# One scatter a head across both halves of the array, fixed score buffers, other row tiles

## The chip, the cores and the metric

The kernel runs on one core of a Trainium2 chip. The metric is the device time of one execution in microseconds. Three executions of the kernel before took 1567.34 us in the median (1565.12 to 1568.61). All traces and profiles here are of one execution on that core.

## The reference

Talking-heads attention (the scores and the attention weights are each mixed over the heads) and then two feed-forward layers, in fp32:

```python
# attention: batch 4, heads 12, sequence 448, head_dim 64
scores = (q @ k.transpose(0, 1, 3, 2)) / sqrt(64)
scores = einsum('bhij,hg->bgij', scores, w_pre)       # mix the 12 heads
attn = softmax(scores, axis=-1)                       # with 1e-9 added to the sum
attn = einsum('bhij,hg->bgij', attn, w_post)          # mix the 12 heads again
x = (attn @ v) laid out as (1792, 768)
# feed-forward, 768 -> 1536 -> 768, then 768 -> 2048 -> 768
x = (sigmoid(x @ w_gate) * (x @ w_val)) @ w_out
h = maximum(x @ w_in, 0)
out = (h * h) @ w_out2
```

## The kernel before

The program has two parts that overlap a little: `attention` (lines 65 to 444) and `mlp` (from line 447 on). The second part multiplies each fp32 matrix as three products of rounded parts (line 692) and keeps TensorE busy without a break once attention is over. The change is in attention alone.

A batch's 448 query rows are cut into four row tiles (`row_tiles`, line 33): 120, 120, 120 and 88 rows. Rows are handled in groups of GI = 10, so that 10 rows x 12 heads = 120 partitions: 12, 12, 12 and 9 groups in the four tiles, 45 a batch, 180 in all.

For each tile, `scores` (line 181) is called once for each of six pairs of heads. TensorE makes the two heads' scores (rows of the tile on the partitions, 448 keys along), ScalarE copies one head and VectorE the other from PSUM to SBUF (tile `e`, three buffers of two heads each), and then DMAs scatter `e` into tile `g`, where the rows of a group and the 12 heads lie on the partitions together: 5 rows x 12 heads = 60 partitions in the lower half of the array (0 to 59) and the other 60 in the upper half (64 to 123). A head has two DMAs, one a half (line 209); each moves 60 rows of 1792 bytes in a full tile, from 60 neighbouring partitions to 5 partitions, at a stride of 12, by 12 columns. Nearly all are issued on SyncE's queue (SP), line 217; some of the first tile's on ScalarE's. The first tile is scattered in two blocks (four columns first; the list `second`, line 375, has the rest). `g` has two buffers, so a tile's scatters wait until the groups of the tile before the last have been read.

The loop over the steps s (line 376 on) takes one group a step. `premix` (line 223, every second step) multiplies two groups of `g` by the pre-mixing weights `wp`, four matmuls a group pair and half; `maximum`, `exponent` and `normal` make the softmax on VectorE, ScalarE and GpSimd; `postmix` (line 269) mixes again; `values` (line 298) multiplies by v when a chunk of two tiles is done. The v tiles come through four buffers by loads on SP's queue (line 295), the fifth and sixth of a chunk when `values` has freed the first two. The results leave by stores on the same queue (line 321). `k` and `q` loads (lines 168, 176) are there as well: SP works its queue in program order.

The scores of a later tile n are spread over the steps by the list `front` (line 338): pair p is due at step a + p (z - a) // 6, where a is two steps before the first group of tile n - 1, and z is LA = 5 steps before the first group of tile n. A pair may also be made earlier, from a on, if the planned TensorE cost leaves room.

`masks` (line 121) and `mixers` (line 145) build the mixing weights once at the start.

Of the kernel before, what the change touches and what calls it, by code (L numbers as in the profile page):

```python
# [7 lines left out]
F32 = mybir.dt.float32  # L8
# [3 lines left out]
ALU = mybir.AluOpType  # L12
# [4 lines left out]
P = 128  # L17
JP = 112
GI = 10
HV = 2  # L20
LAG = 3
LA = 5
NA = 9
HB = GI // 2
HP = P // 2
# [6 lines left out]

def row_tiles(S):

    n = -(-S // (8 * GI)) * 2 * GI
    cuts = [t * n for t in range(4)] + [S]
    return list(zip(cuts, cuts[1:]))


def columns(i0, i1):  # L40

    return 2 * -(-(i1 - i0) // (2 * GI))


def blocks(b, i0, i1):

    n = columns(i0, i1)
    return [(0, 4), (4, n)] if b == i0 == 0 else [(0, n)]
# [16 lines left out]
def attention(tc, q, k, v, w_pre, w_post, xs, B, H, S, D):  # L65
# [10 lines left out]
    nc = tc.nc  # L76
    JT = S // JP
    NP = H // 2
# [3 lines left out]
    for b in range(B):  # L82
        for t, (i0, i1) in enumerate(row_tiles(S)):
            if t % 2 == 0:
                chunks.append([b, i0, i1, len(groups), 0])
            for g0 in range(i0, i1, GI):
                groups.append((len(tiles), g0 - i0, min(GI, i1 - g0), len(chunks) - 1, g0))
            chunks[-1][2] = i1
            chunks[-1][4] = len(groups)
            tiles.append((b, i0, i1 - i0))  # L90
# [3 lines left out]
    GT = IM // GI  # L94
    CM = max(c[2] - c[1] for c in chunks)
    KH = HB * H

    with ExitStack() as ctx, ExitStack() as mid, ExitStack() as left:
        kw = dict(side="right")
# [2 lines left out]
        po = ctx.enter_context(tc.tile_pool(name="a_o", bufs=4, **kw))  # L102
        pp = ctx.enter_context(tc.tile_pool(name="a_p", bufs=1, **kw))
        pa = mid.enter_context(tc.tile_pool(name="a_a", bufs=NA, **kw))
        pg = mid.enter_context(tc.tile_pool(name="a_g", bufs=2, **kw))
        ps_b = ctx.enter_context(tc.tile_pool(name="ps_b", bufs=2, space=PSUM, **kw))
        ps_q = mid.enter_context(tc.tile_pool(name="ps_q", bufs=2, space=PSUM, side="left"))
        ps_m = mid.enter_context(tc.tile_pool(name="ps_m", bufs=4, space=PSUM, side="left"))
# [3 lines left out]
        p0 = left.enter_context(tc.tile_pool(name="a_0", bufs=1, side="left"))  # L112
# [4 lines left out]

        wr = p0.tile([P, 2, H], F32, name="wr")
        mask = p0.tile([P, GI, H], F32, name="mask")

        def masks():
            nc.gpsimd.memset(wr, 0.0)
            nc.gpsimd.memset(mask, 0.0)
            nc.gpsimd.memset(wp, 0.0)
            for n, w in enumerate((w_pre, w_post)):
                for u in range(2):
                    nc.sync.dma_start(
                        out=wr[u * HP : u * HP + KH, n, :],
                        in_=w.unsqueeze(0).to_broadcast([HB, H, H]),
                    )  # L130
            for u in range(2):
                m = mask[u * HP : (u + 1) * HP, u * HB : (u + 1) * HB]
                nc.gpsimd.memset(m, 1.0)
                for base, mult in ((0, 1), (H - 1, -1)):
                    nc.gpsimd.affine_select(
                        out=m,
                        in_=m,
                        compare_op=ALU.is_ge,
                        fill=0.0,
                        base=base,  # L140
                        pattern=[[-mult * H, HB], [0, H]],
                        channel_multiplier=mult,
                    )

        def mixers():
            for u in range(2):
                r = slice(u * HP, (u + 1) * HP)
                x = wp[r, :KH].rearrange("p (i g) -> p i g", g=H)
                nc.vector.tensor_tensor(
                    out=x,  # L150
                    in0=mask[r, u * HB : (u + 1) * HB],
                    in1=wr[r, 0:1, :].to_broadcast([HP, HB, H]),
                    op=ALU.mult,
                )
            nc.vector.tensor_scalar(out=wp, in0=wp, scalar1=SCALE, scalar2=None, op0=ALU.mult)
            nc.vector.tensor_tensor(
                out=wq.rearrange("p g i -> p i g"),
                in0=mask,
                in1=wr[:, 1:2, :].to_broadcast([P, GI, H]),
                op=ALU.mult,  # L160
            )
# [17 lines left out]
        g_t, second = {}, []  # L179

        def scores(n, p):

            b, i0, rows = tiles[n]
            isz = full[n]
            if p == 0:
                g_t[n] = pg.tile([P, GT, S], F32, tag="g", name="g")
            kt = k_t.pop((b, p)) if i0 + rows == S else k_t[b, p]
            ps = [
                ps_q.tile([P, S], F32, tag="q", name="ps_s")
                for _ in range(2)  # L190
            ]
            for o in range(2):
                r = slice(o * D, (o + 1) * D)
                nc.tensor.matmul(  # L194
                    ps[o][:isz], lhsT=q_t[n][r, p, :isz], rhs=kt[r], start=True, stop=True
                )
            if n == 0 and p >= 3:
                e = [pa.tile([IM, S], F32, tag="a", name="e0") for _ in range(2)]
            else:
                t = p4.tile([IM, 2, S], F32, tag="e", name="e")  # L200
                e = [t[:, o] for o in range(2)]
            for o in range(2):
                if o:
                    nc.vector.tensor_copy(e[o][:isz], ps[o][:isz])
                else:
                    nc.scalar.copy(e[o][:isz], ps[o][:isz])  # L206
                e0 = 0
                for m, (g0, g1) in enumerate(blocks(b, i0, i0 + rows)):
                    for y in range(2):
                        e1 = e0 + (g1 - g0) * HB  # L210
                        to = g_t[n][y * HP : y * HP + KH].rearrange("(r h) g j -> h r g j", h=H)
                        move = (to[2 * p + o, :, g0:g1], e[o][e0:e1])
                        if m:
                            second.append(move)
                        else:
                            queue = nc.scalar if n == 0 and o and p in (1, 3, 4, 5) else nc.sync
                            queue.dma_start(out=move[0], in_=move[1])  # L217
                        e0 = e1


        a_t = {}
# [1 line left out]
        def premix(s):  # L223
            n, r0 = groups[s][:2]
            t = r0 // (2 * GI)
            for y in range(2):
                if s + y < NG and groups[s + y][0] == n:
                    a_t[s + y] = ps = ps_m.tile([P, S], F32, tag="m", name="ps_m")
                    r = slice(y * HP, y * HP + KH)
                    for u in range(2):  # L230
                        nc.tensor.matmul(  # L231
                            ps[u * HP : (u + 1) * HP],
                            lhsT=wp[r],
                            rhs=g_t[n][r, 2 * t + u],
                            start=True,
                            stop=True,
                        )
# [87 lines left out]
        starts = [next(s for s in range(NG) if groups[s][0] == n) for n in range(NT)] + [NG]  # L325
# [9 lines left out]

        front = []
        for n in range(1, NT):
            front += [(max(starts[n - 1] - 2, 0), starts[n] - LA, n, p) for p in range(NP)]
        def due(s):

            a, z, _, p = front[0]
            return s >= a + p * (z - a) // NP
# [22 lines left out]
        for p in range(0, NP, 2):  # L365
            q_load(0, p, p + 2)
            load_next(k_load, k_order)
            load_next(k_load, k_order)
        masks()
        for p in range(NP):  # L370
            scores(0, p)
        q_load(1)
        mixers()
        for m, (x, y) in enumerate(second):
            (nc.scalar if m in (3, 7) else nc.sync).dma_start(out=x, in_=y)
        for s in range(NG + 30):
            if s < NG and groups[s][1] // GI % 2 == 0:
                premix(s)
# [412 lines left out]
@with_exitstack  # L791
def whole(ctx, tc, q, k, v, w_pre, w_post, wg, wv, wo, wi2, wo2, out):
    B, H, S, D = k.shape[0], 2 * k.shape[1], k.shape[3], k.shape[2] // 2
    DM = out.shape[0]
    dram = ctx.enter_context(tc.tile_pool(name="dram", bufs=1, space=DRAM))
    xs = [dram.tile([DM, S], F32, name=f"xs{b}") for b in range(B)]
    feed = mlp(tc, xs, wg, wv, wo, wi2, wo2, out, DM, wg.shape[0] * P, wi2.shape[0] * P)
    with tc.manual_schedule():
        need = next(feed)
        for given in attention(tc, q, k, v, w_pre, w_post, xs, B, H, S, D):  # L800
            for _ in range(EACH[given - 1]):
                if need <= given:
                    need = next(feed)
        for _ in feed:
            pass
# [44 lines left out]
```

## Time and profile before

| what | value |
|---|---|
| median of three runs | 1567.34 us |
| profiled execution, its own time | 1565.1 us |
| its span, first to last instruction | 1563.4 us |
| mean granted TensorE clock | 0.976 |
| PE (TensorE matmul) busy | 1471.2 us, 94% of the span |
| VectorE (DVE), ScalarE (ACT), GpSimd (POOL) busy | 802.6, 502.0, 497.7 us |
| chain that ended last | PE 68%, of it line 692 (feed-forward) 64% |
| scatters of a full tile | 264 issues of 105.0 KB each |

The page cuts the span in 40 slices. PE's busy tenths are 5 to 9 in the first 14 slices and 9 from then on; the granted clock is below full in several of the same first 14 slices. Attention fills these slices: the last matmul of the post-mixing starts shortly before 553 us, and the feed-forward part follows. [...]

### The profile page before, as it was taken

How to read it: one execution, taken by the hardware profiler on the slowest of the kernel's cores; microseconds unless marked ns; L12 is line 12 of the kernel's file. 1: busy time of each engine (PE TensorE's matmuls, PEld its weight loads, DVE VectorE, ACT ScalarE, POOL GpSimd, SP SyncE). 2: the span in 40 equal slices, each digit the busy share in tenths (PEclk: the TensorE clock that was granted, in tenths of full speed). 3: DMA queues.
4: the chain of work that ended last, by engine and by line, in shares of the span. 5: the costliest groups of instructions: out<-in, count | busy, mean ns of one | idle time of the engine just before them, and what ended most of it. 6: DMA issues, size and time to landing. Idle time of an engine off the chain costs nothing.

```text
span 1563.4 us, 22405 instructions
## 1 busy us (share of the span) xinstructions
PE 1471.2 (94%) x8208; PEld 1195.5 (76%) x8208; DVE 802.6 (51%) x1366; ACT 502.0 (32%) x1026; POOL 497.7 (32%) x395
## 2 busy tenths in 40 slices
PE   5778898879889899999999999999999999999999
PEld 1444464545546589999999999999999999999998
DVE  2464665656658757777888998951111100333000
ACT  2233333334334533333224443322222211333111
POOL 0121212122112325555455555542222222222221
PEclk9798999989989999999999999999999999999999
DMA  3434435444443435444544445642211121111221
GB/s 109 136 119 142 145 101 153 137 142 137 155 139 114 154 107 193 152 172 162 166 152 167 154 158 186 221 159 63 61 48 55 51 61 51 51 58 50 78 78 42
DMA packets 83305, 186.68 MB, mean 119 GB/s; under 512 B 11708, under 2 KB 49532, under 8 KB 83196
## 3 DMA queue, kind: packets, MB, share of 16 engines
q1 hardware_dynamic: 82906, 184.82, 36.6%
q8 instruction: 65, 1.06, 0.3%
q10 hardware_dynamic: 290, 0.43, 0.1%
q14 instruction: 44, 0.36, 0.1%
HBM read 107.90 MB, written 37.75 MB: 93 GB/s over the span
## 4 chain that ended last, share of the span: by engine, by line
PE 68%; DVE 1%; DMA 1%; ACT 0%; SPq 0%; issue 0%; ACTq 0%; DVEq 0%
PE ps L692 64%; PE ps_p L276 2%; PE ps_v L305 1%; PE ps_m L231 1%; DMA g<-e 0%; PE ps_s L194 0%; DMA vraw<-in_v 0%; DVE ap L288 0%; DVE nm L242 0%; SPq L217 0%; DVE xl L622 0%; ACT xh L621 0%; ACT a L249 0%; DVE sm L257 0%; ACT wn L264 0%
## 5 line engine op out<-in xcount | busy, mean ns | idle before, releaser
L560 POOL TENSOR_TENSOR wl<-w,wh 128x768 fp32r<-128x768 f32 (+1 forms) x140 | 258.0, 1845 | 556.8 <-ACT wh L552 549.4
L692 PE MATMUL ps<-xh,wh 128*128 128x448 f32 x960 | 351.1, 366 | 0.0
L692 PE MATMUL ps<-xh,wl 128*128 128x448 f32 x960 | 350.7, 365 | 0.0
L692 PE MATMUL ps<-xl,wh 128*128 128x448 f32 x960 | 350.6, 365 | 0.0
L692 PE MATMUL ps<-hh,wl 128*128 128x448 f32 x672 | 246.8, 367 | 0.0
L692 PE MATMUL ps<-hl,wh 128*128 128x448 f32 x672 | 246.8, 367 | 0.0
L692 PE MATMUL ps<-hh,wh 128*128 128x448 f32 x672 | 246.7, 367 | 0.0
L276 PEld LDWEIGHTS ps_p<-wn,a 128*112 128x112 f32 x1440 | 163.9, 183 | 97.1 <-issue 60.3
L260 POOL TENSOR_SCALAR wn<-wq,sm 128x120 f32<-128x120 f32 x166 | 97.2, 585 | 402.1 <-DVE sm L257 264.2
L276 PE MATMUL ps_p<-wn,a 128*112 128x120 f32 x1440 | 189.5, 282 | 14.6 <-POOL wn L260 6.1
L692 PEld LDWEIGHTS ps<-xh,wh 128*128 128x128 f32 x960 | 180.3, 188 | 15.5 <-issue 0.9
L692 PEld LDWEIGHTS ps<-xh,wl 128*128 128x128 f32 x960 | 180.3, 188 | 14.5 <-POOL wl L560 0.2
L692 PEld LDWEIGHTS ps<-xl,wh 128*128 128x128 f32 x960 | 180.3, 188 | 14.2
L546 POOL TENSOR_TENSOR w<-w,w_f 128x768 f32<-128x768 f32 (+1 forms) x70 | 135.7, 1938 | 59.0 <-DVE w_f L535 59.0
L242 DVE TENSOR_REDUCE nm<-ps_m 128x1 f32<-128x448 f32 x180 | 111.2, 618 | 78.2 <-PE ps_m L231 78.0
L194 PE MATMUL ps_s<-k,q 64*120 64x448 f32 (+1 forms) x384 | 114.6, 646 | 33.0 <-ACT e L206 27.6
L249 ACT ACTIVATE a<-ps_m,nm 128x448 f32<-128x448 f32 x180 | 114.6, 637 | 71.4 <-DVE sm L254 40.1
L692 PEld LDWEIGHTS ps<-hl,wh 128*128 128x128 f32 x672 | 126.1, 188 | 11.6
L692 PEld LDWEIGHTS ps<-hh,wh 128*128 128x128 f32 x672 | 126.1, 188 | 11.6
L692 PEld LDWEIGHTS ps<-hh,wl 128*128 128x128 f32 x672 | 126.1, 188 | 11.6
L710 DVE TENSOR_TENSOR ps<-ps,sg 128x448 f32<-128x448 f32 x48 | 30.4, 632 | 199.4 <-PE ps L692 199.4
L288 DVE COPY ap<-ps_p 112x480 f32<-112x480 f32 x180 | 115.7, 650 | 28.5 <-PE ps_p L276 25.3
(43 smaller groups left out, 1352.0 us busy)
## 6 DMA issues: line engine op xcount, KB each, us to landing
g<-e SPq DMA_DIRECT2D x264, 105.0 KB
ws<-w SPq DMA_DIRECT2D x58, 384.0 KB
w<-ws SPq DMA_DIRECT2D x58, 384.0 KB
w_raw<-in_wo SPq DMA_DIRECT2D x18, 768.0 KB
w_raw<-in_wi SPq DMA_DIRECT2D x16, 768.0 KB
vraw<-in_v SPq DMA_DIRECT2D x48, 224.0 KB
w_raw<-in_wg SPq DMA_DIRECT2D x12, 768.0 KB
w_raw<-in_wv SPq DMA_DIRECT2D x12, 768.0 KB
```

Of the source, the lines that this page charges most:

```text
L194: nc.tensor.matmul(ps[o][:isz], lhsT=q_t[n][r, p, :isz], rhs=kt[r], start=True, stop=True)
L231: nc.tensor.matmul(ps[u * HP : (u + 1) * HP], lhsT=wp[r], rhs=g_t[n][r, 2 * t + u], start=True, stop=True,)
L242: nc.vector.tensor_reduce(out=nm, in_=ps, op=ALU.max, axis=AX.X, negate=True)
L249: nc.scalar.activation(a, ps, AF.Exp, bias=nm, accum_out=sm)
L260: nc.gpsimd.tensor_scalar(out=wn, in0=wq, scalar1=sm, scalar2=None, op0=ALU.mult)
L276: nc.tensor.matmul(ps[:JP, jt], lhsT=a[:, jt * JP : (jt + 1) * JP], rhs=wn.rearrange("p g i -> p (g i)"), start=True, stop=True,)
L288: nc.vector.tensor_copy(ap[c][:, :, :, g0 - i0 : g0 - i0 + rows], ps[:JP, :, :, :rows])
L305: nc.tensor.matmul(ps[o * D : (o + 1) * D, :w], lhsT=vraw[c, (h + o) // HV][:, (h + o) % HV, jt, :], rhs=ap[c][:, jt, h + o, :w], start=jt ...
L546: nc.gpsimd.tensor_tensor(out=x[:, s], in0=x[:, s], in1=fs.pop(n)[:, s], op=ALU.add)
L560: nc.gpsimd.tensor_tensor(out=lo[:, s], in0=w32.pop(n)[:, s], in1=h[:, s].bitcast(F32), op=ALU.subtract)
L692: nc.tensor.matmul(ps, lhsT=a, rhs=x, start=first and n == 0, stop=last and n == total - 1)
L710: nc.vector.tensor_tensor(out=pv, in0=pv, in1=sg[c], op=ALU.mult)
```

## The change

The lower half's 60 partitions move up by four (G0 = 64 - 60), to 4 to 63, so that the ten rows of a group stand at one stride of 12 partitions from 4 to 123. One DMA then moves a head: 120 rows of 1792 bytes in a full tile, to 10 partitions by 12 columns. Partitions 0 to 3 of `g` are set to zero once, and the pre-mix of the lower half reads partitions 0 to 63, with a weight matrix whose first four rows are zero (mask `first`). `g` becomes two fixed tiles that alternate, in place of a pool's two buffers. The row tiles are 120, 120, 100 and 108 rows (12, 12, 10, 11 groups). LA goes from 5 to 3, and the first step of a tile's scores from two steps to one step before the previous tile's first group. The order of rows within `e` (`row_order`) stays.

```diff
-LA = 5
+LA = 3
@@ row_tiles
-    n = -(-S // (8 * GI)) * 2 * GI
-    cuts = [t * n for t in range(4)] + [S]
+    n = -(-S // (2 * GI))
+    cuts = [0]
+    for t in range(4):
+        cuts.append(min(cuts[-1] + (n // 4 + ((0, 1, 3, 2)[t] < n % 4)) * 2 * GI, S))
@@ attention
+    G0 = HP - KH
...
-        pg = mid.enter_context(tc.tile_pool(name="a_g", bufs=2, **kw))
+        pg = mid.enter_context(tc.tile_pool(name="a_g", bufs=1, **kw))
...
+        first = p0.tile([HP, HB, H], F32, name="first")
+        g_of = [pg.tile([P, GT, S], F32, name=f"g{m}") for m in range(2)]
@@ masks
             nc.gpsimd.memset(wp, 0.0)
-            for n, w in enumerate((w_pre, w_post)):
-                for u in range(2):
-                    nc.sync.dma_start(
-                        out=wr[u * HP : u * HP + KH, n, :],
-                        in_=w.unsqueeze(0).to_broadcast([HB, H, H]),
-                    )
+            for g in g_of:
+                nc.gpsimd.memset(g[:G0], 0.0)
+            nc.sync.dma_start(
+                out=wr[G0 : G0 + GI * H, 0, :], in_=w_pre.unsqueeze(0).to_broadcast([GI, H, H])
+            )
             for u in range(2):
-                m = mask[u * HP : (u + 1) * HP, u * HB : (u + 1) * HB]
+                nc.sync.dma_start(
+                    out=wr[u * HP : u * HP + KH, 1, :],
+                    in_=w_post.unsqueeze(0).to_broadcast([HB, H, H]),
+                )
+            for u, m in ((0, first), (0, mask[:HP, :HB]), (1, mask[HP:, HB:])):
                 nc.gpsimd.memset(m, 1.0)
-                for base, mult in ((0, 1), (H - 1, -1)):
+                lead = G0 if m is first else 0
+                for base, mult in ((-lead, 1), (H - 1 + lead, -1)):
...
@@ scores
-                g_t[n] = pg.tile([P, GT, S], F32, tag="g", name="g")
+                g_t[n] = g_of[n % 2]
...
+                to = g_t[n][G0 : G0 + GI * H].rearrange("(r h) g j -> h r g j", h=H)
                 for m, (g0, g1) in enumerate(blocks(b, i0, i0 + rows)):
-                    for y in range(2):
-                        e1 = e0 + (g1 - g0) * HB
-                        to = g_t[n][y * HP : y * HP + KH].rearrange("(r h) g j -> h r g j", h=H)
-                        move = (to[2 * p + o, :, g0:g1], e[o][e0:e1])
-                        if m:
-                            second.append(move)
-                        else:
-                            queue = nc.scalar if n == 0 and o and p in (1, 3, 4, 5) else nc.sync
-                            queue.dma_start(out=move[0], in_=move[1])
-                        e0 = e1
+                    e1 = e0 + (g1 - g0) * GI
+                    move = (to[2 * p + o, :, g0:g1], e[o][e0:e1])
+                    if m:
+                        second.append(move)
+                    else:
+                        queue = nc.scalar if n == 0 and o and p in (1, 3, 4, 5) else nc.sync
+                        queue.dma_start(out=move[0], in_=move[1])
+                    e0 = e1
@@ premix
-                    r = slice(y * HP, y * HP + KH)
+                    r = slice(y * HP, HP + y * KH)
@@ front
-            front += [(max(starts[n - 1] - 2, 0), starts[n] - LA, n, p) for p in range(NP)]
+            front += [(max(starts[n - 1] - 1, 0), starts[n] - LA, n, p) for p in range(NP)]
```

## Rows read from the trace of the kernel before

**Rows 1.** Windows: us, busy time and count of each engine, PEclk, DMA share, GB/s.

```profile
0.00:549.00 549.00, 460.25 (x3197) 266.50 (x3198) 324.75 (x833) 198.16 (x529) 114.57 (x190) 0.93 0.43 135
331.00:385.00 54.00, 52.49 (x396) 30.92 (x392) 38.21 (x97) 21.30 (x56) 12.72 (x21) 1.00 0.38 118
```

**Rows 2.** Waits of PE's matmuls, 64.3 to 549 us: total, times, longest.

```profile
PE ps_v L305 <- DMA vraw<-in_v: 28.6, 6, 7.5
PE ps_s L194 <- ACT e L206: 18.5, 14, 3.2
PE ps_p L276 <- POOL wn L260: 5.4, 5, 3.1
PE ps_p L276 <- ACT wn L264: 4.2, 4, 2.7
PE ps_p L276 <- DVE ap L288: 3.9, 6, 1.4
```

**Rows 3.** Windows: the stretches at the lower clock (the sum is of eleven after 61 us).

```profile
44.00:61.00 17.00, 10.94 (x40) 5.43 (x40) 5.17 (x12) 3.48 (x9) 1.17 (x2) 0.50 0.41 129
...
sum 55.00, PE 44.04 PEld 24.90 DVE 10.39 ACT 12.20 POOL 6.62; mean PE 4.00 PEld 2.26 DVE 0.94 ACT 1.11 POOL 0.60
```

**Rows 4.** Windows in which little but scatters moves, and one with weight loads.

```profile
174.00:187.00 13.00, 11.45 (x100) 6.73 (x98) 7.68 (x24) 4.60 (x14) 2.86 (x5) 1.00 0.33 123
...
283.00:286.00 3.00, 3.00 (x11) 1.70 (x11) 1.13 (x4) 0.32 (x2) 0.58 (x1) 0.51 0.33 120
...
389.00:392.00 3.00, 3.00 (x16) 0.74 (x16) 0.91 (x4) 1.24 (x5) 1.05 (x2) 0.50 0.98 279
```

**Rows 5.** DMA issues: line's tiles, queue, count, KB each.

```profile
g<-e SPq DMA_DIRECT2D x264, 105.0 KB
```

**Rows 6.** Timeline of SP's queue and of PE, 171 to 201 us.

```profile
171.02 16.52 SPq L217 DMA_DIRECT2D g<-e  x20
187.76 0.34 SPq L321 DMA_DIRECT2D xs<-xo  x1
188.66 0.34 SPq L295 DMA_DIRECT2D vraw<-in_v  x1
...
188.25 0.98 PE L231 MATMUL ps_m<-g,wp 60*64 60x448 f32 x8
195.32 5.82 PE L305 MATMUL ps_v<-ap,vraw 112*64 112x208 f32 x32 [6.09 <-DMA vraw<-in_v]
```

**Rows 7.** Waits of PE's matmuls, 0 to 64.2 us.

```profile
PE ps_m L231 <- DMA g<-e: 10.4, 2, 7.2
PE ps_s L194 <- ACT e L206: 9.1, 7, 4.8
```

**Rows 8.** Timeline of the start, several engines.

```profile
0.79 0.12 POOL L122 MEMSET wr<- 128x24 f32 x1 [0.29 <-POOLq L837]
0.84 0.19 POOL L123 MEMSET mask<- 128x120 f32 x1
...
2.16 0.59 POOL L135 TENSOR_SCALAR_AFFINE_SELECT mask<-mask 64x60 f32<-64x60 f32 x2
...
8.44 16.32 SPq L217 DMA_DIRECT2D g<-e  x16
...
19.39 0.45 DVE L149 TENSOR_TENSOR wp<-mask,wr 64x60 f32<-64x60 f32 x2
19.51 1.53 ACTq L217 DMA_DIRECT2D g<-e  x2
...
25.30 17.24 SPq L375 DMA_DIRECT2D g<-e  x22
...
26.05 1.99 PE L231 MATMUL ps_m<-g,wp 60*64 60x448 f32 x8 [7.24 <-DMA g<-e]
...
44.07 2.45 PE L231 MATMUL ps_m<-g,wp 60*64 60x448 f32 x8 [3.15 <-DMA g<-e]
...
51.33 1.97 PE L194 MATMUL ps_s<-k,q 64*120 64x448 f32 x4 [4.80 <-ACT e L206]
```

**Rows 9.** Waits of SP's queue, 0 to 550 us: total, times, longest.

```profile
SPq L217 <- PE ps_m L231: 15.7, 4, 6.2
```

More of the change, by code (lines that the diff above doesn't have):

```diff
@@ L145, in mixers @@
         def mixers():
-            for u in range(2):
+            for u, m in enumerate((first, mask[HP:, HB:])):
                 r = slice(u * HP, (u + 1) * HP)
@@ L149, in mixers @@
                 nc.vector.tensor_tensor(
[L150 to L153, printed above, removed]
+                    out=x, in0=m, in1=wr[r, 0:1, :].to_broadcast([HP, HB, H]), op=ALU.mult
                 )
```

## The prediction

> **What bounds the kernel now.** The 40 slices of the page come first: from the fifteenth on TensorE (PE) has no idle tenth, and the chain that ended last runs through line 692 there. That is the feed-forward part, which the change doesn't touch. Whatever the change is worth lies in the attention stage before it, so the views after that are of 0 to 549 us: windows, then PE's waits, then the DMA share, then SP's queue.
>
> The windows show PE busy for 460 of these 549 us, so 89 us are idle, while every other engine is far from full; in a stretch without stalls PE reaches 52.5 of 54 us [rows 1]. The bound is PE plus its stalls. The waits name the stalls. After 64 us: 28.6 us for loads of v, 18.5 us for the copies into `e`, 13.5 us for three smaller causes [rows 2]. Before it: 10.4 us directly for scatters and 9.1 us for `e` [rows 7]. Some stalls cost twice: the clock is granted at its lower level in 44 to 61 us and in eleven shorter stretches later, each of them during or just after a stall, and PE is busy in the eleven for 44.0 us, which is 22 us of work at full clock [rows 3].
>
> What stands behind both large waits is one resource. Where scatters move nearly alone, the DMA share stops at 0.33 and the rate at 120 to 123 GB/s, though the same engines reach 0.98 and 279 GB/s a little later [rows 4]. 0.33 of 16 engines is 5.3: a scatter, which goes to five partitions at a stride, seems to be served by five engines, full, while eleven rest. A scatter of 105.0 KB (107.5 kB) [rows 5] at 120 GB/s takes 0.90 us; SP issues one every 0.83 us [rows 6]. So the five engines are the slower of the two, and work piles up in front of them. A v load issued at 188.66 comes behind twenty scatters, which alone held SP from 171 to 187.5, and PE can start on it only at 195.32, 6.7 us later [rows 6]; at the start, with nothing piled up, a scatter issued at about 24.0 (the last of the sixteen) releases PE at 26.05, in 2.0 us [rows 8]. The copies into `e` wait for the same pile: the three buffers are free only when their scatters have read them.
>
> **The change part by part.**
>
> *One scatter a head.* 24 scatters a full tile become 12, each of 120 rows and 215 kB, to ten partitions at a stride. If five engines came from five strided partitions, ten come from ten. At 24 GB/s an engine (120 / 5) the new scatter takes 0.90 us on ten, so a tile takes 10.8 us of them instead of 21.5. Bounds: 0.77 us if it reached the 279 GB/s of the weight loads, 1.79 us if five engines stay. I take 0.90, the rate of the nearest row, since each engine still moves 12 rows.
>
> [...]
>
> *Issues.* 0.83 us each on SP [rows 6], a tile 19.9 us of SP's time before, 10.0 after. Blocks a third of the size cost about the same, 0.77 us each for ACT's two [rows 8], so size does not set it, and I take 0.83. Bounds: 0.34 (a store [rows 6]) to 1.66 (each row stride paid for). At 1.66 SP would be as full as before, and about 12 us of the gain on v loads would be lost.
>
> *Other row tiles, LA, and the first step.* The number of score matmuls, padded rows and scattered rows stays (460 columns of padded rows a batch in both). What moves is the scores' calls. Behind the old tile of nine groups, the next tile's 24 scatters had six steps, about 18 us at 3 us a step (549 / 180), for 21.5 us of the five engines; the shortest span now is eight steps for 10.8 us. The old first step put a scatter in SP's queue before the last group of a nine-group tile had been read, which held SP, with everything behind it, four times for 15.7 us [rows 9]; one step later the read is already issued. The price is a smaller margin: the last pair is due five steps before its use instead of seven, about 13 us, against some 6 us for copies, issues and landing. Hidden; if landing took over 11 us, each of 15 tiles would stall by the difference.
>
> *Fixed buffers, zeros, masks.* Two zero fills of 5376 values a partition on GpSimd: by the fills of 24 and 120 values, 0.79 ns a value, 4.3 us each [rows 8]; with a third mask's 0.7 us GpSimd ends at about 12 us instead of 2.75. VectorE needs the masks at 19.4, so 7 us of cover are left. Bound on the other side: at the rate of the mask selection (0.29 us for 60 values) the fills would take 52 us and delay the start by some 35. I take the fills' own rate: nothing. The lower half's 64 rows instead of 60: nothing, at most 3 us (TensorE streams the same 448 columns).
>
> **The sum**, in the profiled execution's time, 1565.1 us (span 1563.4):
> - Start, 18 us. Sixteen issues held SP until 24.8, though the last copy's scatter on ACT's queue was issued at 19.51; with half as many the first pre-mix starts about 2.1 us after 19.51, at 21.6 instead of 26.05: 4.4. The 22 issues of the second blocks (17.2 us) become ten (8 us), so the wait of 3.15 at 44.07 and the 4.80 at 51.33 behind it go [rows 8], with 1.2 of the other `e` waits. PE's 10.9 us at the lower clock in 44 to 61 [rows 3] shrink by up to 5.5; I take 4.5. (Bounds 8 to 22.)
> - Copies into `e`: 18.5 to about 3, 15.5 us (10 to 18.5).
> - v loads: six waits of 28.6 us [rows 2]. A load then lands some 3 us after its issue, and is issued some 5 us earlier because SP's pile is half as high. Where `values` runs two calls a step, it is asked for only about 4 us ahead, so 1 us may stay of each: 23 us gone (8 to 28.6).
> - GpSimd's `wn`: 5.4, of which the longest, 3.1, sits behind blocked copies: 3 (0 to 5). The other small waits stay.
> - Clock: of the 22 us, 4 stay: 18 (8 to 22), by how many stalls over about 2 us are left.
>
> Together 77.5 us: 1487.6 in this execution's terms. It lies 0.14% below the median of 1567.3; in the median's terms 1490 us. A cross-check: PE's 460 us less the lost clock (22 and about 18 in the first 61 us) are 420 us at full clock; with some 13 us lost to the clock at the start, 12 of idle time there, 3% of idle as in the stall-free stretch, and 13 of small waits, attention ends at about 471 instead of 549: 78 less.
>
> **Rivals.**
> 1. *The engines don't double; only issues halve.* For it: 0.33 may come from a port or a queue and not from the count of partitions. Against it: 5.3 matches five too well. Then v and `e` keep waiting for the same 120 GB/s. The start gains 11 (there SP's issue, not the engines, is the bound), the wider spread of the short tile's scatters a third of the v waits with their clock (10 + 5), 15: 1565.1 - 26 = 1539, in the median's terms 1541; if the later scores eat that, no change.
> 2. *The v load takes the bound's place.* It stands on SP behind a store that waits for ACT's copy (187.76, then 188.66), whatever the scatters do, and ACT has the exponentials ahead of it. Then v gives 5 and the clock 8: 18 + 15.5 + 5 + 3 + 8 = 49.5, or 1516, in the median's terms 1518. Against it: SP's pile, not ACT, held the store [rows 6].
> [...]
>
> **How the numbers follow.** Forecast 0.65 (1470 to 1506 by itself), rival 2 0.20, rival 1 0.10, rival 3 0.05. All waits of rows 2 gone, with start and clock at their upper bounds, give 105 us (60.6 + 22 + 22), 1462.5 in the median's terms, which would need every small wait gone as well; all at their lower bounds 34 (8 + 10 + 8 + 0 + 8), 1533. The range 1466 to 1533 holds forecast and rival 2 and leaves out most of rivals 1 and 3. A difference under 0.2% can't be told from none; of rival 1, 0.03 falls there. Faster 0.92, same 0.03, slower 0.05.
>
> **What would show it.** The DMA share with scatters alone rises to about 0.65 with 240 GB/s while they move; 12 scatters on SP a tile at 0.8 us; first pre-mix at about 21.6 us; the waits for v under 8 us and for `e` under 5 us in total; the lower clock only in the first 40 us or so; attention over at about 471 us; from there on the trace as before, 78 us earlier. It is wrong if the share stays at a third, if v keeps over 15 us, or if the first pre-mix comes later than 26 us because of the zero fills.

## The result, and the profile after

The changed kernel takes 1471.18 us in the median of four runs (1469.80 to 1473.77) against 1566.23 before: a ratio of 0.9393, 95% interval 0.9375 to 0.9412, so 95 us or 6% faster. The prediction was 1490 with a range of 1466 to 1533. The profiled execution took 1471.6 us (span 1469.8), 93.5 us less than that of before. From here on times of profiled executions are compared with each other, and medians with medians.

The page of the changed kernel, parts 1 and 2: busy time of each engine; then, by 40 slices, PE's busy tenths and the granted clock (PEclk, in tenths of full speed).

```profile
PE 1439.8 (98%) x8208; PEld 1178.0 (80%) x8208; DVE 801.7 (55%) x1366; ACT 503.0 (34%) x1026; POOL 508.8 (35%) x400
...
PE   6899999999998999999999999999999999999999
...
PEclk9999999999999999999999999999999999999999
```

PE is busy nine tenths or more from the third slice on, in all slices but one, where it had gaps up to the fourteenth before. Its waits from 64.3 to 549 us, the same view as [rows 2]:

```profile
PE ps_p L281 <- ACT wn L269: 4.2, 4, 2.7
PE ps_s L200 <- ACT e L212: 3.2, 5, 0.7
PE ps_p L281 <- POOL wn L265: 1.7, 3, 0.9
PE ps_p L281 <- DVE ap L293: 1.3, 1, 1.3
PE ps_v L310 <- DMA vraw<-in_v: 0.3, 1, 0.3
```

The waits for v went from 28.6 us to 0.3, those for the copies into `e` from 18.5 to 3.2, and with them the stalls at the lower clock [rows 3]. Windows after: 32 to 455 us at full clock throughout; the stretch 44 to 61 us, which stood at 0.50 before; and the one short stretch left at the lower level, near the end of attention (columns as in [rows 1]; PEclk as a share of full speed).

```profile
32.00:455.00 423.00, 408.43 (x3144) 243.23 (x3143) 315.78 (x816) 192.09 (x514) 113.74 (x177) 1.00 0.55 164
...
44.00:61.00 17.00, 16.32 (x121) 9.65 (x121) 13.28 (x36) 7.64 (x20) 4.67 (x8) 1.00 0.64 179
...
455.00:458.00 3.00, 3.00 (x17) 2.87 (x16) 0.91 (x4) 0.98 (x5) 0.00 (x0) 0.50 0.55 216
```

What a scatter gets now shows in a window in which SP issued nothing else (six scatters, in the fence on SP's queue below), the answer to [rows 4]:

```profile
190.00:194.00 4.00, 3.38 (x25) 1.72 (x25) 2.61 (x7) 1.29 (x4) 1.17 (x2) 1.00 0.63 198
```

0.63 of 16 engines is 10.1, where it was 5.3. The rate in this window is 198 GB/s. At the start, where the second blocks' scatters stand close behind one another, it is 243 GB/s at nearly the same share:

```profile
23.00:26.00 3.00, 3.00 (x12) 0.48 (x6) 0.62 (x1) 0.00 (x0) 0.00 (x0) 1.00 0.65 243
```

So a scatter of 215 kB takes 0.88 to 1.09 us, where the prediction had 0.90: about half the time of before for the same bytes. The prediction inferred ten engines for ten strided partitions from 5.3 of 16 for five; this share agrees.

The packets add a second sign: those in all and under 512 B, those of ScalarE's queue (q10), and the scatters that it issues, first before, then after.

```profile
DMA packets 83305, 186.68 MB, mean 119 GB/s; under 512 B 11708, under 2 KB 49532, under 8 KB 83196
...
q10 hardware_dynamic: 290, 0.43, 0.1%
...
g<-e ACTq DMA_DIRECT2D x8, 35.0 KB
g<-e ACTq DMA_DIRECT2D x2, 70.0 KB
```

```profile
DMA packets 83302, 186.65 MB, mean 127 GB/s; under 512 B 11708, under 2 KB 49532, under 8 KB 83196
...
q10 hardware_dynamic: 380, 0.57, 0.1%
...
g<-e ACTq DMA_DIRECT2D x4, 70.0 KB
g<-e ACTq DMA_DIRECT2D x2, 140.0 KB
```

There are 204 scatters instead of 408, and yet as many small packets. ScalarE's queue, which carries scatters alone, gives the number for one. Before, its ten scatters have 240 rows of 1792 bytes, and the other 50 of the 290 packets have 4 bytes each: five a scatter. After, its six have 320 rows and 60 packets of 4 bytes: ten a scatter. By that, 408 x 5 and 204 x 10 are the same 2040, and the count stays as it was. The number of small packets of a scatter, five and ten, goes with the shares of 5.3 and 10.1 engines.

The chain behind a v load, SP's queue and PE at a like place as [rows 6] (x6 counts instructions merged in one line; in brackets, below, the idle time before an instruction and what ended it):

```profile
188.04 7.42 SPq L222 DMA_DIRECT2D g<-e  x6
...
198.41 0.37 SPq L326 DMA_DIRECT2D xs<-xo  x1
198.87 0.38 SPq L300 DMA_DIRECT2D vraw<-in_v  x1
...
203.04 3.53 PE L310 MATMUL ps_v<-ap,vraw 112*64 112x240 f32 x32
```

Six scatters in 7.4 us with pauses, in place of twenty in 16.5 without one; the load goes out earlier than it is wanted, and PE runs through.

The start, the answer to [rows 8]:

```profile
1.06 9.09 POOL L131 MEMSET g<- 4x5376 f32 x2
...
11.89 0.59 POOL L144 TENSOR_SCALAR_AFFINE_SELECT mask<-mask 64x60 f32<-64x60 f32 x2
...
19.42 0.20 DVE L158 TENSOR_TENSOR wp<-first,wr 64x60 f32<-64x60 f32 x1
19.53 0.78 ACTq L222 DMA_DIRECT2D g<-e  x1
...
22.70 1.77 PE L236 MATMUL ps_m<-g,wp 64*64 64x448 f32 x8 [3.87 <-DMA g<-e]
...
34.31 0.98 PE L236 MATMUL ps_m<-g,wp 64*64 64x448 f32 x8
...
44.58 0.98 PE L236 MATMUL ps_m<-g,wp 64*64 64x448 f32 x8
```

The zero fills take 9.1 us of GpSimd, which ends at 12.5; VectorE starts on the masks at 19.42 (19.39 before), so the fills cost nothing. The first pre-mix comes at 22.70 (21.6 was foreseen, 26.05 before), the third at 34.31 (44.07 before, [rows 8]), the fifth at 44.58; of before, this is the fifth:

```profile
64.26 0.98 PE L231 MATMUL ps_m<-g,wp 60*64 60x448 f32 x8
```

From 455 us on the trace runs as before from 549.

### The profile page after: what moved, and what is told of

Read it like the earlier page. It is cut to its first block, busy times and chain, and to the rows that moved or that the text cites. A ratio compares the mean times of both kernels' runs of the same rounds, so it can differ in the third digit from the quotient of the medians.

```text
span 1469.8 us, 22024 instructions
## 1 busy us (share of the span) xinstructions
PE 1439.8 (98%) x8208; PEld 1178.0 (80%) x8208; DVE 801.7 (55%) x1366; ACT 503.0 (34%) x1026; POOL 508.8 (35%) x400
## 4 chain that ended last, share of the span: by engine, by line
PE 77%; DVE 1%; ACT 0%; issue 0%; ACTq 0%
PE ps L697 68%; PE ps_p L281 4%; PE ps_v L310 2%; PE ps_m L236 2%; PE ps_s L200 1%; DVE ap L293 0%; DVE xl L627 0%; DVE nm L247 0%; ACT xh L626 0%; ACT e L212 0%; ACT wn L269 0%; DVE sm L262 0%; ACT a L254 0%; ACT o L729 0%; DVE sm L259 0%
## 5 line engine op out<-in xcount | busy, mean ns | idle before, releaser
L281 PEld LDWEIGHTS ps_p<-wn,a 128*112 128x112 f32 x1440 | 158.2, 178 | 85.9 <-issue 40.6
L281 PE MATMUL ps_p<-wn,a 128*112 128x120 f32 x1440 | 183.1, 276 | 10.5 <-ACT wn L269 4.2
L697 PEld LDWEIGHTS ps<-xh,wh 128*128 128x128 f32 x960 | 180.3, 188 | 15.5 <-issue 0.9
L557 ACT CAST wh<-w 128x768 fp32r<-128x768 f32 (+1 forms) x140 | 113.4, 813 | 33.4 <-POOL w L551 33.4
```

The costliest lines, as they stand in the source:

```text
L281: nc.tensor.matmul(ps[:JP, jt], lhsT=a[:, jt * JP : (jt + 1) * JP], rhs=wn.rearrange("p g i -> p (g i)"), start=True, stop=True,)
L557: nc.scalar.copy(h[:, s], w32[n][:, s])
L697: nc.tensor.matmul(ps, lhsT=a, rhs=x, start=first and n == 0, stop=last and n == total - 1)
```

## The experiments

Theory: five full engines were the bound behind the waits, and ten engines are the gain. Rivals: the number of issues on SP; the order (tiles, due steps). Ratios are to the kernel before in the same job, with 95% intervals. A cut of rows or columns below always moves the same bytes.

**e1, one scatter with the old order.**

```diff
 # the changed kernel with
-LA = 3
+LA = 5
 # row_tiles of before (120, 120, 120, 88), and in front:
-(max(starts[n - 1] - 1, 0), ...
+(max(starts[n - 1] - 2, 0), ...
```

> One scatter a head (ten strided partitions) with the row tiles, LA and first step of before. Theory (the scatter's engines: it is served by as many engines as it has strided partitions, and five full engines made the pile): 1473 to 1490 us, nearly the whole gain of 95, DMA share over 0.6 while scatters move. Rival (the order: tiles and due steps carry most of the gain): 1520 us or more. Rival (issues on SP): the same as the theory.

Measured: 1512.74 us, ratio 0.9638 (0.9612 to 0.9663): outside what the theory gave, and short of the rival's bound. But e1 is not "the scatter alone". With fixed buffers the old first step puts a tile's scatters, in program order, ahead of the last read of their buffer behind a nine-group tile, so the pre-mix of that tile's last group takes rows of a later tile, and has to wait for them. The pool had made SP wait there instead, 15.7 us [rows 9]. PE's waits show it:

```profile
PE ps_m L234 <- DMA g<-e: 16.3, 3, 5.7
```

Three waits of over 5 us, with the clock at its lower level around each (0.51 in 136 to 143, 252 to 262 and 379 to 389 us). So e1 does not compute the attention above, the first step belongs to the fixed buffers, and e5 asks the question again.

**e2, the order alone.**

```diff
 # the kernel before with
-LA = 5
+LA = 3
 # row_tiles as changed (120, 120, 100, 108), and in front:
-(max(starts[n - 1] - 2, 0), ...
+(max(starts[n - 1] - 1, 0), ...
```

> The kernel before with only the new row tiles, LA = 3 and the later first step; two scatters a head stay. Theory (engines): 1535 to 1560 us, the share stays at a third, v and e still wait. Rival (the order): under 1510 us. Rival (issues): as the theory, since the issues stay.

Measured: 1549.08 us, ratio 0.9888 (0.9873 to 0.9904), inside the theory's range: 18 us of the 95. PE's waits from 64 to 540 us, two of the lines:

```profile
PE ps_v L307 <- DMA vraw<-in_v: 24.4, 6, 6.8
PE ps_s L196 <- ACT e L208: 3.7, 6, 0.9
```

v still waits, as the theory had it, but `e` does not: its waits fall from 18.5 us [rows 2] to 3.7 with five engines still. For `e`, the order alone is enough.

**e3, ten engines with the old number of issues.**

```diff
-    return [(0, 4), (4, n)] if b == i0 == 0 else [(0, n)]
+    return [(0, 4), (4, n)] if b == i0 == 0 else [(0, n // 2), (n // 2, n)]
...
-                    if m:
+                    if m and n == 0:
                         second.append(move)
```

> The changed kernel with each head's scatter split in two by columns (6 and 6, or 5 and 5), so 24 issues a tile as before, but each to ten strided partitions. Theory (engines): 1471 to 1485 us; SP's queue as full as before, the waits for v and e stay small. Rival (issues): back to 1530 to 1565 us.

Measured: 1495.32 us, ratio 0.9543 (0.9525 to 0.9561). Most of the gain is there without fewer issues, so the rival falls; but 24 us are missing, and the result lies 10 us above the theory's range. (The first tile is left as in the changed kernel, with 24 scatters where the kernel before has 48, so the start keeps its fewer issues. In all there are 384 scatters, against 408 before and 204 in the changed kernel.) PE waits 9.9 us for v again. SP's queue and PE in e3:

```profile
195.46 10.13 SPq L222 DMA_DIRECT2D g<-e  x12
...
206.22 3.22 SPq L222 DMA_DIRECT2D g<-e  x4
...
210.53 0.38 SPq L300 DMA_DIRECT2D vraw<-in_v  x1
...
214.86 3.00 PE L310 MATMUL ps_v<-ap,vraw 112*64 112x240 f32 x16 [3.65 <-DMA vraw<-in_v]
```

PE can now start on the load 4.3 us after its issue, where it took 6.7 before [rows 6], but it is issued late, behind sixteen scatters. (In the changed kernel the same load goes out at 198.87.) SP's time is a second resource, which the engines' pile had hidden.

**e4, eight and two partitions.**

```diff
-                    move = (to[2 * p + o, :, g0:g1], e[o][e0:e1])
+                    c0 = e0 + (g1 - g0) * 8
+                    moves = [
+                        (to[2 * p + o, :8, g0:g1], e[o][e0:c0]),
+                        (to[2 * p + o, 8:, g0:g1], e[o][c0:e1]),
+                    ]
...
+                        second.extend(moves)
```

> The changed kernel with each head's scatter split in two by rows, eight and two strided partitions. Theory, if the engines used are always the same first ones: two engines get the rows of both, as many bytes each as the five had before, so 1525 to 1560 us though eight engines take part. Rival (any free engines serve, the total counts): 1471 to 1490 us. Rival (issues): 1530 to 1565 us; e3 tells it from the theory.

Measured: 1544.69 us, ratio 0.9861 (0.9841 to 0.9880). This is the theory's range. There are as many issues a tile as in e3 (the first tile is split as well, so it has 24 scatters more than in e3), and yet it is no better than e2.

The packet records of the trace (start and size of each packet) show how many engines are full. A load of v has 112 packets of 2048 bytes; spread evenly over 16 engines that would be seven for each, and the counts below are multiples of seven. The load issued at 118.20 behind scatters has 98 packets under way by 2.11 us after its issue, and then none until 3.94. 98 is 14 x 7: two engines are held up and fourteen are free. The same break at 98, a pause of over 0.5 us, stands in eight more loads of e4. Two engines with more work than the others are what comes out if the two partitions' DMA goes to engines that already have a share of the eight; ten different ones would have had 12 rows of a head each. So here the most loaded engines decided, not how many took part: 1544.69 us, against 1495.32 in e3. By the 98 packets the engines of both DMAs overlap; which engines they are is not in the trace.

**e5, one scatter with the old tiles and LA.**

```diff
 # the changed kernel with LA = 5 and row_tiles of before; the first step stays as changed
```

> As e1 (one scatter a head, tiles of 120, 120, 120, 88, LA = 5), but with the new first step, one step before the previous tile's first group, so that no scatter of a tile stands in the program ahead of the last read of its buffer. Theory (engines): the waits of PE for g in e1 (16.3 us, three of over 5 us, each with the lower clock behind it) came from that place alone, so 1472 to 1485 us. Rival (the row tiles carry a large part): 1495 us or more.

Measured: 1479.00 us, ratio 0.9453 (0.9438 to 0.9469); PE waits 0.8 us for v and for `g` after the start not at all. This is the middle of the theory's range, and e1's loss came from the first step. The tiles with LA give the last 9 us.

**e6, LA alone.**

```diff
-LA = 3
+LA = 5
```

> The changed kernel with LA = 5 again (new tiles, new first step). Theory: with twelve issues a tile on ten engines the due step matters little: 1468 to 1478 us. Rival (LA = 3 spreads the scatters away from the v loads): 1485 us or more, with waits for v over 8 us.

Measured: 1474.96 us, ratio 0.9422 (0.9406 to 0.9437). This is what the theory gave. Its interval overlaps that of the changed kernel: LA is worth some 4 us by the ratios, and perhaps nothing.

**e7, the halves on two queues.**

```diff
 # e3 with
                         queue = nc.scalar if n == 0 and o and p in (1, 3, 4, 5) else nc.sync
+                        if n and not o:
+                            queue = nc.scalar
```

> As e3 (24 scatters a tile of half the size, ten partitions each), but the scatters of the head that ScalarE copies are issued on ScalarE's queue, so SP has 12 a tile again. Theory 2 (after e3: SP's issue time is the second resource, because v loads stand behind scatters in its queue): back to 1470 to 1482 us, v waits under 4 us. Rival (the number of DMAs costs by itself, on the engines or by landing): stays at 1490 to 1500 us. A risk for both: ScalarE's exponentials come later by its issues, some 0.8 us each.

Measured: 1483.29 us, ratio 0.9475 (0.9460 to 0.9490): 1 us outside the theory's range, well under the rival's. The waits for v are gone, as foreseen, and 12 us remain; one new wait of 3.72 us stands at the start, where SP takes 12.90 us to issue the ten second blocks of the first tile (9.52 in e10), while ScalarE issues scatters of the next tile. Why SP pauses there was not isolated.

```profile
37.99 1.77 PE L238 MATMUL ps_m<-g,wp 64*64 64x448 f32 x8 [3.72 <-DMA g<-e]
```

**e8, six buffers for v in the kernel before.**

```diff
-        pv4 = ctx.enter_context(tc.tile_pool(name="a_v", bufs=4, **kw))
+        pv4 = ctx.enter_context(tc.tile_pool(name="a_v", bufs=6, **kw))
...
-            if s in (4, 5, 6, 7):
+            if s in range(4, 10):
...
-                    if x[1] + 2 + 4 * HV <= H:
+                    if x[1] + 2 + 6 * HV <= H:
```

> The kernel before with six buffers for v instead of four, so that all six loads of a chunk are made ahead; scatters stay as they were. Theory (the pile delays v by landing late, and that wait with its clock is a term of its own): waits for v from 28.6 us to under 3, some 25 to 40 us gained, 1527 to 1545 us, and the waits for e stay. Rival (e takes over: what PE doesn't lose to v it loses to the copies): 1555 us or more.

Measured: 1539.14 us, ratio 0.9829 (0.9811 to 0.9846), 27 us, inside the theory's range. PE's waits from 64 us, the first two:

```profile
PE ps_s L194 <- ACT e L206: 19.7, 12, 3.6
PE ps_v L305 <- ACT xo L320: 8.0, 2, 5.4
```

The waits for v are gone, those for `e` stay (18.5 before), and a new one of 8.0 us comes from results whose stores are late (ScalarE's copies wait 12.9 us for them). So v was a term of its own, and the pile has other ways to PE.

**e9, five and five partitions.**

```diff
 # as e4, cut at 5
+                    c0 = e0 + (g1 - g0) * 5
```

> The changed kernel with each head's scatter split in two by rows, five and five strided partitions; order, tiles and fixed buffers stay as changed. It differs from e3 only in the engines that a scatter gets. Theory (engines): 1540 to 1555 us, near e2 and e4, so that e3 minus this is the engines' share, some 50 us. Rival (e2 and e4 were slow for another reason, the old buffers or two engines alone): under 1520 us.

Measured: 1547.16 us, ratio 0.9886 (0.9851 to 0.9920), inside the theory's range. From the second tile on everything but the engines is as in e3, and the picture of before is back: a window with scatters, then SP's queue and PE.

```profile
106.00:118.00 12.00, 11.39 (x90) 5.57 (x90) 5.75 (x17) 4.87 (x14) 2.33 (x4) 1.00 0.35 122
```

```profile
103.94 13.01 SPq L227 DMA_DIRECT2D g<-e  x16
...
117.99 0.34 SPq L305 DMA_DIRECT2D vraw<-in_v  x1
...
125.41 3.46 PE L315 MATMUL ps_v<-ap,vraw 112*64 112x240 f32 x16 [6.08 <-DMA vraw<-in_v]
```

A third of the engines, 122 GB/s, and a v load that is waited for until 7.4 us after its issue. The packets of this load say which engines: 77, or 11 x 7, are under way by 1.88 us after its issue, then none until 4.03. Eleven engines are free and five are held up. The kernel before has the same break at 77 in eleven of its v loads (that of [rows 6] has the 77 by 2.10 us); the changed kernel has one at 42, or 6 x 7, in its first load. So all these scatters go to the same five engines, and after the change to ten.

How much is the engines? The expectation says that e9 differs from e3 in the engines only, but e9 splits the first tile's scatters too, 24 more issues than e3. The fifth pre-mix, e9 first, then e3:

```profile
61.11 0.98 PE L241 MATMUL ps_m<-g,wp 64*64 64x448 f32 x8
46.49 0.98 PE L236 MATMUL ps_m<-g,wp 64*64 64x448 f32 x8
```

Of the 53 us between the two profiled executions (54 by the ratios, 0.9886 and 0.9543), 15 are lost up to this point, to the engines and the added issues together. The other 38 come where the number and the size of the issues are the same, and are the engines' alone.

**e10, e3 with six buffers for v.**

```diff
 # e3 with the three edits of e8
```

> As e3 (24 scatters a tile of half the size, ten partitions each, all on SP), with six buffers for v, so that its loads are made ahead. Theory 2 (e3 lost 24 us because v loads came late behind scatters on SP): waits for v from 9.9 us to under 2, 1477 to 1486 us. Rival (the doubled count costs elsewhere): 1488 to 1500 us.

Measured: 1483.82 us, ratio 0.9473 (0.9443 to 0.9502): within the theory's range. v's lateness is 11 of the 24 us that the doubled issues cost; 12 remain. Two stretches at the lower clock that the changed kernel has not:

```profile
41.00:45.00 4.00, 4.00 (x18) 1.52 (x18) 3.23 (x9) 1.79 (x6) 0.58 (x1) 0.57 0.42 131
332.00:338.00 6.00, 6.00 (x26) 4.80 (x24) 2.69 (x6) 1.90 (x6) 0.72 (x2) 0.50 0.61 183
```

Each follows a wait of PE for `e`, of 1.9 and of 3.9 us; ahead of the second there is also one of 3.0 us for a result's copy. The 10 us of PE work in them lose some 5, and PE's waits are 8.6 us more in sum than in the changed kernel, which together is about the rest. Why those copies come late there was not isolated.

## Why the prediction was right, and where its sizes were off

- **The bound, five engines.** Right, and shown: the breaks at 77 and 42 of 112 packets count five and ten engines, and e9 against e3 gives the engines 38 us at equal issues, and a part of 15 more at the start. Rival 1 fell with the share of 0.63.
- **Ten engines at 0.90 us a scatter.** Ten is right, and 0.90 lies inside the 0.88 to 1.09 that the two windows give. It matters little, since a tile's twelve scatters take 11 to 13 us of the engines in some 30.
- **Issues at 0.83 us.** Right: two scatters take 1.64 us of SP, 0.82 each, with twice the rows. Behind the start, what the prediction gave them was only the way for v. e3 against the changed kernel puts the halved issues at 24 us (0.9543 to 0.9393), of which e10 shows 11 to be v.
- **`e` and the order.** The prediction put the waits for `e` down to the engines' pile. The size came out (15.3 us), but the pile is only one way to it: e2 clears these waits by the order with five engines, e5 by ten engines with the old tiles (3.7 us left in both). Order and tiles are worth 18 us by themselves (e2), 9 on top of the new scatter (e5 against the changed kernel); the gains overlap. The prediction had no term for the order of its own.
- **First step.** It was counted for SP's wait alone [rows 9]; e1 shows that with fixed buffers it is needed for the kernel to compute the same. Left as it was, it costs 29 us (0.9638 against e5's 0.9453).
- **Zero fills, 64 rows.** Nothing, as foreseen: the fills are hidden, and eight pre-mix matmuls take 0.98 us with 60 rows (64.26) and with 64 (44.58).
- **Rival 2**, a v load held by the store ahead of it, did not come: that wait is 0.3 us. Its form shows in e3 instead, with scatters in the store's place. Rival 3 had 0.05, on a slower kernel; no run shows a ground for it, and the runs showed a share of 0.63 and a ratio of 0.9393 instead.

**The sum: 77.5 foreseen, 93.5 measured** (profiled executions). The start gave 19.7 (64.26 to 44.58 at the fifth pre-mix) for 18. From there to the last matmul of the post-mixing PE has the same 3098 matmuls, first before, then after:

```profile
64.26:552.94 488.68, 425.46 (x3098) 254.52 (x3098) 309.66 (x797) 187.66 (x504) 109.76 (x172) 0.94 0.43 138
44.58:459.16 414.58, 402.47 (x3098) 241.43 (x3098) 308.86 (x797) 188.33 (x504) 110.82 (x172) 1.00 0.55 162
```

Its busy time falls by 23.0, with the granted clock from 0.94 to 1.00; that is the clock's term, for 18. Its idle time falls from 63.2 to 12.1, by 51.1: v 28.3 for 23; `e` 15.3 for 15.5; `wn` 3.0 for 3; and two waits that were to stay, `ap` 2.6 and results' copies 2.2, for 0. Together 93.8. The mechanism was right and these terms were too small: v by 5.3 (1 us was left for each load), the clock by 5.0 (4 us were left), the small waits by 4.8, the start by 1.7. In the cross-check, which gave 471 us for the end of attention and not 459, 3% of idle time and 13 us of small waits stand beside each other; the 12.1 us that are left are 3% of this stretch, small waits included.

Not tried: twelve issues on five engines, for which no form of the scatter was at hand. So the value of fewer issues is known only with ten engines, and 12 of its 24 us are located (waits for copies, lower clock) but not explained.

## What to carry to other kernels

Look at the DMA share in a window in which one kind of transfer runs. Here a plateau at 0.33, or five of the 16 engines, with transfers piling up behind it, said that the transfer's shape and not its bytes set the rate, and scatters of the same bytes to ten strided partitions in place of five lifted it to 0.63. The packets of a v load told the same: of its 112, 35 (5/16) came late behind scatters to five partitions (e9), and 14 (2/16) behind those to eight and two (e4). Then look for the queue behind it: here the issue time on SP was the next resource, worth 24 us more. The stalls of PE here were paid twice, by 51 us of idle time and 23 of the clock; both went nearly whole with the pile, where the forecast had kept a rest of each.

## What the runs showed of the hardware that was not expected

- Two DMAs on eight and two strided partitions were as slow as two on five (1544.69 and 1547.16 us), though the first held up two engines (14 of 112 packets late) and the second five (35).
- A scatter's issue took SP 0.83 us with 60 rows (16.52 for twenty) and 0.82 with 120 (1.64 for two), while a store took 0.37.
- An engine moved about 23 GB/s in scatters when five were at work (120 GB/s over 5.3), and 20 to 23 when ten were (198 over 10.1 in 190 to 194 us, 243 over 10.4 in 23 to 26).
- A load behind a pile on five engines was not held up whole: 77 of its 112 packets went at once and 35 waited (e9, 118 us); behind a pile on two engines 98 and 14 (e4).
